# Strassen weight combinations on VectorE in portions, a re-dealt last round, and a later start for the second token group's operands

## The chip, the cores and the metric

The kernel runs on one core of one Trainium2 chip. The metric is the device time of one execution in microseconds. Three runs of the kernel before took 757.85, 758.66 and 759.13 us; the median is 758.66 us. One more execution was profiled, and all rows below come from it.

## The reference

An attention with packed queries makes 2304 rows of 512 values; two feed-forward networks follow, the first with softplus, the second with x·sigmoid(x). Everything is float32.

```python
p_packed = sm_attn(p, k, v)                 # per batch and head
x = sm_attn(q, p_packed, p_packed)          # then [2304, 512]
h = x @ moe_w_in                            # 512 -> 2048
x = softplus(h) @ moe_w_out                 # 2048 -> 512
h = x @ moe2_w_in
out = (h * sigmoid(h)) @ moe2_w_out
```

## The kernel before, in words

Each float32 operand of a large product is split into a high part (rounded to the matmul's fp32r format by a ScalarE copy) and a low part (the difference, by VectorE); a product is three matmuls: low×high, high×low, high×high.

The first 380 us do the attention and the first network. The second network (`second`) runs in 24 steps, `step(k)`: 8 steps for each of three groups of 768 tokens, which is two blocks of 384. Its input product is a Winograd-Strassen scheme with seven products Q1 to Q7 per step (`products`, L900, six matmuls each), into four PSUM tiles pA, pB, pC and pD. Several products accumulate into one tile with VectorE or ScalarE reading the tile in between: pA receives Q1, is read as `ta` (L1091), then receives Q2; pB receives Q6, is read by VectorE as `u2` (rows show `tu`), then receives Q7; pC receives Q5, is read for `c2`, then receives Q3. So a late reader stops TensorE. The order on TensorE in a step is Q1, Q6, output 0, Q2, Q7, output 1, Q5, output 2, Q3, Q4, output 3. An output is a 12-matmul block of the output product two steps earlier (`out_tile`, L1039).

The seven operand tiles of a token group's x lie in the pools `xc0` and `xc1` (alternating). `x_high` (ScalarE, L569), `x_low` (VectorE, L573) and `x_sum` (VectorE, L566) fill them in the last two steps before the group's first step; the table `plans` in `plan_second` gives each piece a step and a point. `xc1` is opened in the place of the pool `stage` when step 6 begins, and `stage` holds the last converted weights (`whl`) until their DMA to the scratch tensor `wd` (`store_i`, L237) has read them.

For the last group the output product is also a Strassen scheme. Its weight combinations are computed once: eight tiles of 128 × 2048 are loaded from `od` (`t_load`, L804), combined by GpSimd (`t_sums`, L808: one sum over 128 × 1024, then four differences over 128 × 256), split (`t_high` on ScalarE, L817; `t_low` on VectorE, L821) and stored to `td` (`t_store`, L825). `T_AT` gives each tile its step (16 is added) and says whether it follows `T_EARLY` or `T_LATE`, the tables of points. Tiles 0 to 5 use the pool `tw`, the others the first 512 columns of `ya`.

A point is a place in the program text of a step: L, A0 and D0 stand after `u2`, D1, A1 and M after Q7 and the low part of g11, D2 after the first read of pC, A2 after output 2, S before output 3's add, A3 and D3 at the end. All engines execute in program order, SyncE's DMA issues too, so a piece at a point waits behind what is written before it and holds up what is written after.

From step 18 on, fourteen output blocks per pair of steps (`out_group`, L965, six matmuls; seven accumulators in two halves d) are added into `ya` by `add_group` (L976, GpSimd's part L977). A block uses one of four PSUM banks, so TensorE runs at most four blocks ahead of the adds. The sums of the second operand (`s_sum` L941, `s_high` L945, `s_low` L949) are GpSimd's and ScalarE's in the steps. After step 23 the last sums and the last fourteen blocks (f = 3) follow; here `add_group` combines the accumulators: GpSimd adds Q1 to Q6 and Q2, Q5 to Q3, Q6 to Q7 and Q3; VectorE adds the PSUM block, and for Q7 makes two outputs by operations on `ya` alone; each finished output is sent by SyncE (L983).

```python
elif q == Q1:
    vec(a[q], y, a[q])
    gps(a[Q6], a[Q6], a[Q1])
    gps(a[Q2], a[Q2], a[Q1])
```

Of the kernel before, what the change touches and what calls it, by code (L numbers as in the profile page):

```python
# [13 lines left out]
ALU = mybir.AluOpType  # L14
# [4 lines left out]
B, H, S, D = 4, 8, 576, 64  # L19
# [8 lines left out]
D1 = D + 1  # L28
# [13 lines left out]
NQ = 7  # L42
RI = 5
Q1, Q6, Q2, Q7, Q5, Q3, Q4 = range(NQ)
# [5 lines left out]
def body(ctx, tc, kT, vv, qT, pT, wi1, wo1, wi2, wo2, out):  # L50
    nc = tc.nc
# [744 lines left out]
    B_OF = {Q1: (0, 0), Q2: (1, 0), Q3: (1, 1)}  # L796

    def t_load(n):
        if n < 6:
            t = st["tw"].tile([P, 4, DM], F32, name="tw", bufs=5)  # L800
        else:
            t = ya[:, :, :DM]
        ts[n] = t.rearrange("p (c h) (a n) -> p c h a n", c=2, a=2), t
        nc.sync.dma_start(out=t, in_=od[:, n * 4 * DM:(n + 1) * 4 * DM].rearrange("p (c n) -> p c n", c=4))  # L804

    def t_sums(n):
        w, t = ts[n][0][:, :, 0], ts[n][0][:, :, 1]
        op = lambda o, a, b, op: nc.gpsimd.tensor_tensor(out=o, in0=a, in1=b, op=op)  # L808
        at = lambda i: t[:, i[0], i[1]]
        op(w, w, t, ALU.add)  # L810
        op(at(T1), w[:, 0, 1], w[:, 0, 0], ALU.subtract)
        op(at(T3), w[:, 1, 1], w[:, 0, 1], ALU.subtract)
        op(at(T2), w[:, 1, 1], at(T1), ALU.subtract)
        op(at(T4), at(T2), w[:, 1, 0], ALU.subtract)

    def t_high(n):
        nc.scalar.activation(out=ts[n][0][:, :, 0].bitcast(F32R), in_=ts[n][0][:, :, 1], func=AF.Copy)  # L817
# [6 lines left out]
        v = td[:, n * 4 * DM:(n + 1) * 4 * DM].rearrange("p (c n) -> p c n", c=4)  # L824
        nc.sync.dma_start(out=v, in_=ts.pop(n)[1])  # L825

    T_AT = (-8, 0), (-8, 1), (-7, 1), (-6, 0), (-5, 0), (-5, 1), (-4, 0), (-1, 0)
    T_EARLY = (0, "M", t_load), (1, "D0", t_sums), (1, "A2", t_high), (1, "D3", t_low), (2, "A0", t_store)
    T_LATE = (0, "S", t_load), (1, "D2", t_sums), (2, "A0", t_high), (2, "D1", t_low), (2, "M", t_store)

    ring_s = {}

# [11 lines left out]
    def plan_second():  # L844
        for n in range(NJ):
            s, late = T_AT[n]
            s += SO * NJ
            for ds, point, fn in T_LATE if late else T_EARLY:
                fill(s + ds, point, fn, n)
        for jp in range(4, NJ):  # L850
            k = jp - 2
            for n in 2 * jp, 2 * jp + 1:
                fill(k - 1, "M", load_raw, "i", n, 0)
                fill(k, "A0", scale_raw, "i", n, True)
                fill(k, "D0", plain_i, n, True)
            fill(k, "D1", sums_i)
            fill(k, "A1", high_i, 0, 4)
            fill(k, "A1", high_i, 4, NQ)
            fill(k, "D2", low_i, 0, 4)
            fill(k, "D2", low_i, 4, NQ)  # L860
            fill(k, "S", store_i, jp)
        for s in range(1, NSUP):
            plans = {
                (0, "D0"): ((x_high, Q1), (x_high, Q2)),
                (0, "D1"): ((x_high, Q4), (x_low, Q1)),
                (0, "D2"): ((x_low, Q2), (x_low, Q4)),
                (0, "D3"): ((x_sum, Q5),),
                (1, "D0"): ((x_high, Q5), (x_sum, Q7)),
                (1, "D1"): ((x_low, Q5), (x_sum, Q6), (x_high, Q7), (x_high, Q6)),
                (1, "D2"): ((x_low, Q7), (x_low, Q6)),  # L870
                (1, "D3"): ((x_sum, Q3),),
                (2, "D0"): ((x_high, Q3),),
                (2, "D1"): ((x_low, Q3),),
            }
            for (h, point), fns in plans.items():
                for fn, q in fns:
                    fill(NJ * s - 2 + h, point, fn, s, q)

    def second():
# [1 line left out]
        pb = pool("pb", 1, space=PSUM)  # L881
        tmp = st["tmp"]
        slots = [*range(6)]
        units, opnd, saved, later = [], {}, {}, {}
        tw_stack = ExitStack()
        G = None
        gs1, frees = {}, {}
# [46 lines left out]
        def s_sum(k, q, eng):  # L934
            g11, c12, c2 = saved[k]
            s1, s2 = sum_of(Q5), sum_of(Q6)
            a, b, op = {
                Q5: (c2[:, 0], c2[:, 1], ALU.add), Q7: (g11, c2[:, 0], ALU.subtract),
                Q6: (s1, g11, ALU.subtract), Q3: (c12, s2, ALU.subtract),
            }[q]  # L940
            eng.tensor_tensor(out=sum_of(q), in0=a, in1=b, op=op)  # L941
# [8 lines left out]

        def acc(q, d):
            n = 2 * OUT_ORDER.index(q) + d
            c = n // 4 * N1
            return ya[:, n % 4, c:c + N1]

# [16 lines left out]
        def add_group(f, n, y):  # L972
            i, d = divmod(n, 2)
            q = OUT_ORDER[i]
            a = {x: acc(x, d) for x in OUT_ORDER}
            vec = lambda o, x, z, op=ALU.add: nc.vector.tensor_tensor(out=o, in0=x, in1=z, op=op)  # L976
            gps = lambda o, x, z, op=ALU.add: nc.gpsimd.tensor_tensor(out=o, in0=x, in1=z, op=op)  # L977
            yout = lambda t, h: ya[:, 2 * h + d, (2 * SO + t) * N1:(2 * SO + t + 1) * N1]

            def send(t, h):  # L980
                c = (2 * SO + t) * N1
                dm = 2 * h + d
                nc.sync.dma_start(out=out[dm * P:(dm + 1) * P, c:c + N1], in_=yout(t, h))  # L983

            if not f:
                if d:
                    nc.vector.tensor_copy(a[q], y)
                else:
                    nc.scalar.activation(out=a[q], in_=y, func=AF.Copy)
            elif f < NPASS - 1:  # L990
                vec(a[q], y, a[q])
            elif q == Q1:
                vec(a[q], y, a[q])
                gps(a[Q6], a[Q6], a[Q1])
                gps(a[Q2], a[Q2], a[Q1])
            elif q == Q4:
                vec(a[q], y, a[q])
            elif q == Q5:
                vec(a[q], y, a[q])
                gps(a[Q3], a[Q3], a[Q5])  # L1000
            elif q == Q6:
                vec(a[q], y, a[q])
                gps(a[Q7], a[Q7], a[Q6])
                later.setdefault(Q6, []).append(lambda: gps(a[Q3], a[Q3], a[Q6]))
                if d:
                    for fn in later.pop(Q6):
                        fn()
            elif q == Q7:
                vec(a[q], y, a[q])
                vec(yout(1, 0), a[q], a[Q4], ALU.subtract)  # L1010
                send(1, 0)
                vec(yout(1, 1), a[q], a[Q5])
                send(1, 1)
            elif q == Q3:
                vec(yout(0, 1), y, a[q])
                send(0, 1)
            else:
                vec(yout(0, 0), y, a[q])
                send(0, 0)
# [199 lines left out]
                open_xc(1, side="right", reuse_waits="tile")  # L1219
            step(k)  # L1220
        k = NSTEP
        for q in Q5, Q6:
            s_sum(k - 1, q, nc.vector)
            s_high(k - 1, q)
            s_low(k - 1, q, nc.vector)
        for q in Q7, Q3:
            s_sum(k - 1, q, nc.gpsimd)
            s_high(k - 1, q)
            s_low(k - 1, q, nc.gpsimd)
        for k in NSTEP, NSTEP + 1:  # L1230
            for n in range(NQ):
                group_of(k, n)

    setup()
    with tc.manual_schedule():
# [53 lines left out]
```

## Time and profile before

| What | Value |
|---|---|
| Median of three runs | 758.66 us |
| The profiled execution's own time | 758.51 us |
| Its span, first to last instruction | 756.7 us |
| TensorE busy | 739.3 us, 98% of the span |
| VectorE busy | 531.6 us, 70% |
| ScalarE busy | 382.8 us, 51% |
| GpSimd busy | 126.4 us, 17% |
| Mean granted TensorE clock | 0.995 of full speed |

The profiled execution takes 1.8 us longer than its span and lies 0.15 us under the median. Busy shares are averages over very different stages; what matters for a change is which wait ended last at the place that it touches.

### The profile page before, as it was taken

How to read it: one execution, taken by the hardware profiler on the slowest of the kernel's cores; microseconds unless marked ns; L12 is line 12 of the kernel's file. 1: busy time of each engine (PE TensorE's matmuls, PEld its weight loads, DVE VectorE, ACT ScalarE, POOL GpSimd, SP SyncE). 2: the span in 40 equal slices, each digit the busy share in tenths (PEclk: the TensorE clock that was granted, in tenths of full speed). 3: DMA queues.
4: the chain of work that ended last, by engine and by line, in shares of the span. 5: the costliest groups of instructions: out<-in, count | busy, mean ns of one | idle time of the engine just before them, and what ended most of it. 6: DMA issues, size and time to landing. Idle time of an engine off the chain costs nothing.

```text
span 756.7 us, 13739 instructions
## 1 busy us (share of the span) xinstructions
PE 739.3 (98%) x5440; PEld 704.9 (93%) x5440; DVE 531.6 (70%) x962; ACT 382.8 (51%) x723; POOL 126.4 (17%) x116
## 2 busy tenths in 40 slices
PE   8999999999999999999999999999989999999996
PEld 6777889999999999999999998999989999999995
DVE  3888887879877997897556775755467675445555
ACT  3677786656555565565445453333434333543430
POOL 0000000000000000000000000045363035466546
PEclk9999999999999999999999999999999999999998
DMA  9965033145444352567268888689999677987732
GB/s 338 339 218 183 1 140 113 56 181 189 178 165 181 140 195 85 205 241 271 61 234 320 349 290 322 231 288 345 355 392 318 233 257 252 340 268 241 228 108 84
DMA packets 55744, 169.01 MB, mean 223 GB/s; under 512 B 5248, under 2 KB 23168, under 8 KB 52608
## 3 DMA queue, kind: packets, MB, share of 16 engines
q1 hardware_dynamic: 55680, 168.13, 62.5%
q8 instruction: 43, 0.70, 0.4%
q14 instruction: 21, 0.17, 0.1%
HBM read 131.93 MB, written 36.18 MB: 222 GB/s over the span
## 4 chain that ended last, share of the span: by engine, by line
PE 85%; DMA 4%; ACT 4%; DVE 3%; issue 1%; POOL 1%; SPq 1%; DVEq 0%; ACTq 0%; POOLq 0%
PE y L527 24%; PE y L1039 16%; PE h L487 12%; PE pC L900 6%; PE y L965 6%; PE pB L900 6%; PE pA L900 6%; PE pD L900 3%; DMA wraw<-wo 3%; PE psa L453 2%; PE y L520 2%; DMA wd<-whl 2%; POOL ya L977 1%; PE psa L360 1%; DVE ya L976 1%
## 5 line engine op out<-in xcount | busy, mean ns | idle before, releaser
L527 PE MATMUL y<-gh,w 128*128 128x288 f32 x960 | 212.1, 296 | 0.3 <-DVE ya L542 0.2
L527 PEld LDWEIGHTS y<-gh,w 128*128 128x128 f32 x960 | 160.3, 188 | 13.0 <-issue 5.5
L1039 PE MATMUL y<-G,w 128*128 128x384 f32 x768 | 143.2, 334 | 0.0
L527 PE MATMUL y<-gl,w 128*128 128x288 f32 x480 | 141.8, 295 | 0.1
L1039 PEld LDWEIGHTS y<-G,w 128*128 128x128 f32 x768 | 134.0, 188 | 0.0
L487 PE MATMUL h<-ax,vw 128*128 128x288 f32 x768 | 125.0, 298 | 0.3 <-DVE ax L436 0.3
L808 POOL TENSOR_TENSOR tw<-tw 128x256 f32<-128x256 f32 (+1 forms) x30 | 36.9, 1245 | 525.4 <-DMA yT<-ya 498.9
L487 PEld LDWEIGHTS h<-ax,vw 128*128 128x128 f32 x768 | 109.3, 188 | 2.4 <-DVE ax L436 0.5
L527 PEld LDWEIGHTS y<-gl,w 128*128 128x128 f32 x480 | 90.2, 188 | 0.5 <-DVE gl L504 0.5
L499 ACT ACTIVATE gt<-h 128x288 f32<-128x288 f32 x120 | 48.5, 404 | 68.6 <-PE h L487 64.0
L504 DVE TENSOR_TENSOR gl<-gt,gh 128x288 fp32r<-128x288 f32 x120 | 54.1, 451 | 25.1 <-ACT gh L500 24.3
L900 PE MATMUL pB<-xc,w 128*128 128x384 f32 x288 | 57.9, 335 | 2.0 <-DVE tu L1073 1.9
L900 PE MATMUL pC<-xc,w 128*128 128x384 f32 x288 | 57.7, 334 | 1.8 <-DVE c L1073 1.8
L1157 ACT ACTIVATE tc<-tc 128x384 f32<-128x384 f32 x24 | 12.6, 526 | 90.6 <-DVE tc L1073 90.6
L900 PE MATMUL pA<-xc,w 128*128 128x384 f32 x288 | 57.8, 335 | 0.1
L1073 DVE TENSOR_TENSOR tu<-ta,pB 128x384 f32<-128x384 f32 x48 | 26.5, 551 | 42.9 <-PE pB L900 38.2
L500 ACT ACTIVATE gh<-gt 128x288 fp32r<-128x288 f32 x120 | 53.4, 445 | 3.8
L900 PEld LDWEIGHTS pB<-xc,w 128*128 128x128 f32 x288 | 50.5, 188 | 2.7 <-DVE tu L1073 2.7
L900 PEld LDWEIGHTS pC<-xc,w 128*128 128x128 f32 x288 | 50.5, 188 | 2.2 <-DVE c L1073 2.2
L544 DVE TENSOR_TENSOR ya<-y,ya 128x288 f32<-128x288 f32 x104 | 46.8, 451 | 7.2 <-PE y L527 7.0
L900 PEld LDWEIGHTS pA<-xc,w 128*128 128x128 f32 x288 | 50.5, 188 | 0.4 <-ACT ta L1091 0.4
L1052 DVE TENSOR_TENSOR ya<-y,ya 128x384 f32<-128x384 f32 x48 | 26.6, 554 | 25.4 <-PE y L1039 25.3
(122 smaller groups left out, 1098.0 us busy)
## 6 DMA issues: line engine op xcount, KB each, us to landing
w<-wd SPq DMA_DIRECT2D x84, 512.0 KB, 4.8
w<-od SPq DMA_DIRECT2D x32, 512.0 KB, 6.8
wd<-whl SPq DMA_DIRECT2D x8, 1792.0 KB, 7.1
wraw<-wi SPq DMA_DIRECT2D x16, 512.0 KB, 5.6
wraw<-wo SPq DMA_DIRECT2D x16, 512.0 KB, 6.3
raw<-wi SPq DMA_DIRECT2D x16, 512.0 KB, 6.1
raw<-wo SPq DMA_DIRECT2D x16, 512.0 KB, 6.8
od<-ohl SPq DMA_DIRECT2D x16, 512.0 KB, 3.1
```

The costliest lines, as they stand in the source:

```text
L487: nc.tensor.matmul(h, lhsT=w, rhs=x, start=(i == 0), stop=(i == len(mm) - 1))
L499: nc.scalar.activation(out=gt, in_=h, func=AF.Softplus)
L500: nc.scalar.activation(out=gh, in_=gt, func=AF.Copy)
L504: nc.vector.tensor_tensor(out=gl, in0=gt, in1=gh.bitcast(F32), op=ALU.subtract)
L527: nc.tensor.matmul(y, lhsT=w[:, c], rhs=g, start=(j == js[0] and m == 0), stop=(j == js[-1] and m == 2))
L544: nc.vector.tensor_tensor(out=acc, in0=y, in1=acc, op=ALU.add)
L808: op = lambda o, a, b, op: nc.gpsimd.tensor_tensor(out=o, in0=a, in1=b, op=op)
L900: nc.tensor.matmul(out, lhsT=a, rhs=b, start=start and not i, stop=not start and i == len(mm) - 1, skip_group_check=True,)
L965: nc.tensor.matmul(y, lhsT=w[:, j, a, c], rhs=g[:, h], start=(j == m == 0), stop=(j == 1 and m == 2))
L1039: nc.tensor.matmul(y, lhsT=a[:, c], rhs=G[:, g, h, j], start=(k % 2 == j == m == 0), stop=(k % 2 == j == 1 and m == 2),)
L1052: nc.vector.tensor_tensor(out=acc, in0=y, in1=acc, op=ALU.add)
L1073: add = lambda o, i, j, op=ALU.add: nc.vector.tensor_tensor(out=o, in0=i, in1=j, op=op)
```

## The change

Four edits stand in the diff. First, `t_sums` is cut into `t_plain`, `t_sums1` and `t_sums2`, all on VectorE instead of GpSimd, each at a point of its own; `T_AT`, `T_EARLY` and `T_LATE` are new, and tiles 3, 6 and 7 lie in `ya` (tile 3 lay in `tw`; `t_load(n)` for the other five uses `tw`). Second, `plans` begins the x operands of the second and third token group at D2 of the step two ahead, not at D0 (for the second group that is step 6). Third, after step 23 the sums and low parts of Q6, Q7 and Q3 are dealt anew: GpSimd keeps one sum, VectorE takes the rest and does them between its adds; GpSimd's `Q2 += Q1` of the second half goes to the end of its row. Fourth, the accumulators of the last group's outputs are moved round by eight places in `ya`, which goes with the places of the tiles.

```diff
--- before.py
+++ after.py
@@ -796,22 +796,29 @@
     B_OF = {Q1: (0, 0), Q2: (1, 0), Q3: (1, 1)}
 
     def t_load(n):
-        if n < 6:
+        if n not in (3, 6, 7):
             t = st["tw"].tile([P, 4, DM], F32, name="tw", bufs=5)
         else:
             t = ya[:, :, :DM]
         ts[n] = t.rearrange("p (c h) (a n) -> p c h a n", c=2, a=2), t
         nc.sync.dma_start(out=t, in_=od[:, n * 4 * DM:(n + 1) * 4 * DM].rearrange("p (c n) -> p c n", c=4))
 
-    def t_sums(n):
+    def t_op(o, a, b, op=ALU.subtract):
+        nc.vector.tensor_tensor(out=o, in0=a, in1=b, op=op)
+
+    def t_plain(n):
         w, t = ts[n][0][:, :, 0], ts[n][0][:, :, 1]
-        op = lambda o, a, b, op: nc.gpsimd.tensor_tensor(out=o, in0=a, in1=b, op=op)
-        at = lambda i: t[:, i[0], i[1]]
-        op(w, w, t, ALU.add)
-        op(at(T1), w[:, 0, 1], w[:, 0, 0], ALU.subtract)
-        op(at(T3), w[:, 1, 1], w[:, 0, 1], ALU.subtract)
-        op(at(T2), w[:, 1, 1], at(T1), ALU.subtract)
-        op(at(T4), at(T2), w[:, 1, 0], ALU.subtract)
+        t_op(w, w, t, ALU.add)
+
+    def t_sums1(n):
+        w, t = ts[n][0][:, :, 0], ts[n][0][:, :, 1]
+        t_op(t[:, 0, 0], w[:, 0, 1], w[:, 0, 0])
+        t_op(t[:, 0, 1], w[:, 1, 1], w[:, 0, 1])
+
+    def t_sums2(n):
+        w, t = ts[n][0][:, :, 0], ts[n][0][:, :, 1]
+        t_op(t[:, 1, 0], w[:, 1, 1], t[:, 0, 0])
+        t_op(t[:, 1, 1], t[:, 1, 0], w[:, 1, 0])
 
     def t_high(n):
         nc.scalar.activation(out=ts[n][0][:, :, 0].bitcast(F32R), in_=ts[n][0][:, :, 1], func=AF.Copy)
@@ -824,9 +831,15 @@
         v = td[:, n * 4 * DM:(n + 1) * 4 * DM].rearrange("p (c n) -> p c n", c=4)
         nc.sync.dma_start(out=v, in_=ts.pop(n)[1])
 
-    T_AT = (-8, 0), (-8, 1), (-7, 1), (-6, 0), (-5, 0), (-5, 1), (-4, 0), (-1, 0)
-    T_EARLY = (0, "M", t_load), (1, "D0", t_sums), (1, "A2", t_high), (1, "D3", t_low), (2, "A0", t_store)
-    T_LATE = (0, "S", t_load), (1, "D2", t_sums), (2, "A0", t_high), (2, "D1", t_low), (2, "M", t_store)
+    T_AT = (-8, 0), (-8, 1), (-7, 0), (-6, 0), (-6, 1), (-5, 0), (-4, 0), (0, 0)
+    T_EARLY = (
+        (0, "M", t_load), (1, "D0", t_plain), (1, "D1", t_sums1), (1, "D2", t_sums2),
+        (1, "A2", t_high), (1, "S", t_low), (2, "A0", t_store),
+    )
+    T_LATE = (
+        (0, "S", t_load), (1, "D2", t_plain), (1, "S", t_sums1), (2, "D0", t_sums2),
+        (2, "A1", t_high), (2, "D2", t_low), (2, "S", t_store),
+    )
 
     ring_s = {}
 
@@ -861,14 +874,13 @@
             fill(k, "S", store_i, jp)
         for s in range(1, NSUP):
             plans = {
-                (0, "D0"): ((x_high, Q1), (x_high, Q2)),
-                (0, "D1"): ((x_high, Q4), (x_low, Q1)),
-                (0, "D2"): ((x_low, Q2), (x_low, Q4)),
-                (0, "D3"): ((x_sum, Q5),),
-                (1, "D0"): ((x_high, Q5), (x_sum, Q7)),
-                (1, "D1"): ((x_low, Q5), (x_sum, Q6), (x_high, Q7), (x_high, Q6)),
-                (1, "D2"): ((x_low, Q7), (x_low, Q6)),
-                (1, "D3"): ((x_sum, Q3),),
+                (0, "D2"): ((x_high, Q1), (x_high, Q4)),
+                (0, "S"): ((x_low, Q1), (x_low, Q4)),
+                (0, "A3"): ((x_high, Q2),),
+                (1, "D0"): ((x_sum, Q5), (x_sum, Q7), (x_low, Q2)),
+                (1, "D1"): ((x_sum, Q6), (x_high, Q6), (x_high, Q5)),
+                (1, "D2"): ((x_high, Q7), (x_low, Q6), (x_low, Q5)),
+                (1, "S"): ((x_low, Q7), (x_sum, Q3)),
                 (2, "D0"): ((x_high, Q3),),
                 (2, "D1"): ((x_low, Q3),),
             }
@@ -881,7 +893,7 @@
         pb = pool("pb", 1, space=PSUM)
         tmp = st["tmp"]
         slots = [*range(6)]
-        units, opnd, saved, later = [], {}, {}, {}
+        units, opnd, saved, later = [], {}, {}, []
         tw_stack = ExitStack()
         G = None
         gs1, frees = {}, {}
@@ -950,6 +962,7 @@
 
         def acc(q, d):
             n = 2 * OUT_ORDER.index(q) + d
+            n = (n + 8) % 14
             c = n // 4 * N1
             return ya[:, n % 4, c:c + N1]
 
@@ -992,7 +1005,10 @@
             elif q == Q1:
                 vec(a[q], y, a[q])
                 gps(a[Q6], a[Q6], a[Q1])
-                gps(a[Q2], a[Q2], a[Q1])
+                if not d:
+                    gps(a[Q2], a[Q2], a[Q1])
+                else:
+                    later.append(lambda: gps(a[Q2], a[Q2], a[Q1]))
             elif q == Q4:
                 vec(a[q], y, a[q])
             elif q == Q5:
@@ -1001,9 +1017,9 @@
             elif q == Q6:
                 vec(a[q], y, a[q])
                 gps(a[Q7], a[Q7], a[Q6])
-                later.setdefault(Q6, []).append(lambda: gps(a[Q3], a[Q3], a[Q6]))
+                later.insert(d, lambda: gps(a[Q3], a[Q3], a[Q6]))
                 if d:
-                    for fn in later.pop(Q6):
+                    for fn in later:
                         fn()
             elif q == Q7:
                 vec(a[q], y, a[q])
@@ -1219,17 +1235,25 @@
                 open_xc(1, side="right", reuse_waits="tile")
             step(k)
         k = NSTEP
-        for q in Q5, Q6:
-            s_sum(k - 1, q, nc.vector)
-            s_high(k - 1, q)
-            s_low(k - 1, q, nc.vector)
-        for q in Q7, Q3:
-            s_sum(k - 1, q, nc.gpsimd)
-            s_high(k - 1, q)
-            s_low(k - 1, q, nc.gpsimd)
-        for k in NSTEP, NSTEP + 1:
-            for n in range(NQ):
-                group_of(k, n)
+        s_sum(k - 1, Q7, nc.gpsimd)
+        s_sum(k - 1, Q5, nc.vector)
+        s_high(k - 1, Q5)
+        s_sum(k - 1, Q6, nc.vector)
+        s_high(k - 1, Q7)
+        s_low(k - 1, Q5, nc.vector)
+        s_high(k - 1, Q6)
+        s_sum(k - 1, Q3, nc.vector)
+        s_high(k - 1, Q3)
+        group_of(k, 0)
+        s_low(k - 1, Q6, nc.vector)
+        group_of(k, 1)
+        s_low(k - 1, Q7, nc.vector)
+        group_of(k, 2)
+        s_low(k - 1, Q3, nc.vector)
+        for n in range(3, NQ):
+            group_of(k, n)
+        for n in range(NQ):
+            group_of(k + 1, n)
 
     setup()
     with tc.manual_schedule():
```

How the instructions stand, at three places. ScalarE, steps 6 and 7, from `ta` of step 6 (`xc` are the second group's operands, `tg` and `tc` the step's own activations). Before:

```order
L1091 ACTIVATE ta<-pA 128x384
L569 ACTIVATE xc_5806<-ya 128x768 x2
L1115 ACTIVATE tg_5814<-pA 128x384
L1116 ACTIVATE G<-tg_5814 128x384
L569 ACTIVATE xc_5806<-ya 128x768
L1157 ACTIVATE tc_5815<-tc_5815 128x384
```

Now:

```order
L1107 ACTIVATE ta<-pA 128x384
L1131 ACTIVATE tg_5814<-pA 128x384
L1132 ACTIVATE G<-tg_5814 128x384
L569 ACTIVATE xc_5806<-ya 128x768 x2
L1173 ACTIVATE tc_5815<-tc_5815 128x384
L1174 ACTIVATE G<-tc_5815 128x384
L1177 ACTIVATE c_5816<-c_5816 128x768
L1179 ACTIVATE G<-c_5816 128x768
L569 ACTIVATE xc_5806<-ya 128x768
```

The first two splits now follow the activations of g11 (`tg` and `G<-tg`) instead of preceding them; the third has moved to the end of the step.

VectorE, from the end of step 11 into step 12 (`tw` are the weight tiles, `tu` is the first or second read of pB, `c` a read of pC or pD). Before:

```order
L1073 TENSOR_TENSOR G<-tc_6692,G 128x384
L1052 TENSOR_TENSOR ya<-y,ya 128x384
L1073 TENSOR_TENSOR G<-c_6693,G 128x768
L821 TENSOR_TENSOR tw<-tw 128x2x512
L1073 TENSOR_TENSOR tu_6836<-ta,pB 128x384
L1052 TENSOR_TENSOR ya<-y,ya 128x384
L1073 TENSOR_TENSOR tu_6837<-ta,pB 128x384
```

Now:

```order
L1089 TENSOR_TENSOR G<-tc_6546,G 128x384
L828 TENSOR_TENSOR ya<-ya 128x2x512
L807 TENSOR_TENSOR tw<-tw 128x256 x2
L1089 TENSOR_TENSOR G<-c_6547,G 128x768
L1089 TENSOR_TENSOR tu_6691<-ta,pB 128x384
L807 TENSOR_TENSOR tw<-tw 128x256 x2
L807 TENSOR_TENSOR tw<-tw 128x2x512
L1068 TENSOR_TENSOR ya<-y,ya 128x384
L1089 TENSOR_TENSOR tu_6692<-ta,pB 128x384
```

The low part of a weight tile (L821, now L828) no longer stands between the last low part of step 11 and the first read of pB; portions of the combinations stand before and behind that read.

VectorE after step 23 (`sums` by L941 are the operand sums, `G` and `xs` by L949 their low parts, `ya<-y,ya` the adds of blocks). Before:

```order
L941 TENSOR_TENSOR sums<-c_8351 128x384
L949 TENSOR_TENSOR G<-sums,G 128x384
L941 TENSOR_TENSOR sums<-sums,tg_8349 128x384
L949 TENSOR_TENSOR G<-sums,G 128x384
L976 TENSOR_TENSOR ya<-y,ya 128x384 x9
L976 TENSOR_TENSOR ya<-ya 128x384 x2
```

Now:

```order
L953 TENSOR_TENSOR sums<-c_8350 128x384
L953 TENSOR_TENSOR sums<-sums,tg_8348 128x384
L961 TENSOR_TENSOR G<-sums,G 128x384
L953 TENSOR_TENSOR sums<-tc_8349,sums 128x384
L989 TENSOR_TENSOR ya<-y,ya 128x384
L961 TENSOR_TENSOR xs<-sums,xs 128x384
L989 TENSOR_TENSOR ya<-y,ya 128x384
L961 TENSOR_TENSOR G<-sums,G 128x384
L989 TENSOR_TENSOR ya<-y,ya 128x384
L961 TENSOR_TENSOR xs<-sums,xs 128x384
L989 TENSOR_TENSOR ya<-y,ya 128x384 x6
L989 TENSOR_TENSOR ya<-ya 128x384 x2
```

VectorE now does one more sum and two more low parts here, dealt between the first four adds; GpSimd's ten additions of accumulators follow its one sum directly.

## Rows read from the trace of the kernel before

**Rows 1.** The page, part 1: busy time, share of the span and instructions of each engine.
```profile
PE 739.3 (98%) x5440; PEld 704.9 (93%) x5440; DVE 531.6 (70%) x962; ACT 382.8 (51%) x723; POOL 126.4 (17%) x116
```
**Rows 2.** Waits of TensorE: releaser, us in total, times, longest.
```profile
PE y L965 <- DVE ya L976: 3.6, 3, 1.8
PE pB L900 <- DVE tu L1073: 1.9, 1, 1.9
PE pC L900 <- DVE c L1073: 1.8, 1, 1.8
```
**Rows 3.** Chain of waits, 540 to 575 us: start, us, what.
```profile
557.74 2.08 PE y L1039 x12
```
**Rows 4.** Timeline, steps 5 and 6: start, us, instructions [idle before, releaser].
```profile
445.19 1.55 DVE L221 TENSOR_TENSOR wf<-wf 128x256 f32<-128x256 f32 x4
...
454.08 0.95 DVE L1073 TENSOR_TENSOR G<-c,G 128x768 fp32r<-128x768 f32 x1
...
461.89 1.58 ACT L569 ACTIVATE xc<-ya 128x768 fp32r<-128x768 f32 x2 [6.75 <-DMA wd<-whl]
...
462.77 2.25 PE L1039 MATMUL y<-G,w 128*128 128x384 f32 x12
...
466.25 0.54 DVE L1073 TENSOR_TENSOR c<-tu,pC 128x384 f32<-128x384 f32 x1
...
466.85 1.31 PE L900 MATMUL pC<-xc,w 128*128 128x384 f32 x6 [1.83 <-DVE c L1073]
```
**Rows 5.** Timeline, steps 12 and 13.
```profile
551.45 2.79 DVE L1073 TENSOR_TENSOR G<-c,G 128x768 fp32r<-128x768 f32 x1 [3.00 <-ACT G L1163]
...
553.27 1.20 PE L900 MATMUL pA<-xc,w 128*128 128x384 f32 x6
554.16 1.74 DVE L821 TENSOR_TENSOR tw<-tw 128x1024 fp32r<-128x1024 f32 x1
...
556.43 1.31 PE L900 MATMUL pB<-xc,w 128*128 128x384 f32 x6 [1.95 <-DVE tu L1073]
...
571.10 1.20 PE L900 MATMUL pA<-xc,w 128*128 128x384 f32 x6
...
572.40 1.31 PE L900 MATMUL pB<-xc,w 128*128 128x384 f32 x6
...
574.69 1.22 DVE L821 TENSOR_TENSOR tw<-tw 128x1024 fp32r<-128x1024 f32 x1
```
**Rows 6.** GpSimd's instructions by line and shape: count | busy, mean ns | idle before.
```profile
L808 POOL TENSOR_TENSOR tw<-tw 128x1024 f32<-128x1024 f32 x6 | 14.4, 2402 | 524.5 <-DMA yT<-ya 498.9 <-DMA tw<-od 23.3 <-DMA w<-od 2.3
```
**Rows 7.** DMA issues, 490 to 600 us: count, KB each, median us to landing.
```profile
tw<-od SPq DMA_DIRECT2D x6, 1024.0 KB, 7.9
...
ya<-od SPq DMA_DIRECT2D x1, 1024.0 KB, 8.8
td<-ya SPq DMA_DIRECT2D x1, 1024.0 KB, 7.3
```
**Rows 8.** A 20 us window: engines' busy us (count), granted clock, DMA share, GB/s.
```profile
520.00:540.00 20.00, 20.00 (x117) 20.00 (x117) 7.53 (x12) 8.48 (x16) 9.68 (x8) 1.00 1.01 399
```
**Rows 9.** Timeline from the end of step 23.
```profile
730.59 2.76 PE L965 MATMUL y<-xs,w 128*128 128x384 f32 x15
...
732.87 0.56 DVE L976 TENSOR_TENSOR ya<-y,ya 128x384 f32<-128x384 f32 x1 [0.32 <-PE y L965]
...
734.39 0.53 ACT L945 ACTIVATE G<-sums 128x384 fp32r<-128x384 f32 x1 [1.61 <-DVE sums L941]
...
737.65 4.95 PE L965 MATMUL y<-G,w 128*128 128x384 f32 x27 [0.66 <-DVE ya L976]
...
740.61 10.30 POOL L977 TENSOR_TENSOR ya<-ya 128x384 f32<-128x384 f32 x10
...
748.04 2.02 DVE L976 TENSOR_TENSOR ya<-ya 128x384 f32<-128x384 f32 x2
...
751.73 1.94 DVE L976 TENSOR_TENSOR ya<-y,ya 128x384 f32<-128x384 f32 x4
```

## The prediction

> **What bounds the kernel now.** I read the page first: TensorE is busy for 739.3 of 756.7 us [rows 1], so a change that leaves its instructions alone can only win back idle time, some 17 us, most of it in the start that this diff does not touch. The waits of TensorE [rows 2] name what is left in the second network: reads of pB and pC by VectorE, and the adds of the last round. The chain of waits gives the unit: 12 matmuls take 2.08 us [rows 3], so six take 1.04, a step 7 × 1.04 + 4 × 2.08 = 15.6 us. Then the timelines show where each wait comes from.
>
> *Step 6.* Output 1 begins at 462.77 and should hand over to Q3 into pC at 464.85; Q3 begins at 466.85, and its six matmuls show 1.31 busy instead of the usual 1.20 [rows 4, 5]: 2.0 + 0.1 = 2.1 us lost. VectorE read pC only at 466.25, because ScalarE had stood for 6.75 us before two operand splits, until the weights' DMA out of the place of `xc1` had landed at 461.89 [rows 4]; the activations that VectorE needs stand behind those splits.
>
> *Steps 12 and 13.* Q2 begins at 553.27, so Q7 into pB is due at 554.31 and begins at 556.43: 2.1 + 0.1 = 2.2 us. At the second place it is due at 572.14 and begins at 572.40: 0.3 + 0.1 = 0.4 us [rows 5]. What is late there is VectorE: a low part of 128 × 768 took 2.79 us where the same form took 0.95 in step 6 [rows 4, 5], and a weight tile's low part 1.74 us where it took 1.22 later [rows 5]. Both slow ones fall on GpSimd's combinations, whose large sum holds for 2.40 us [rows 6].
>
> *The last round.* Step 23's last twelve matmuls begin at 730.59, so the fourteen blocks begin at 732.67 and need 14.6 us, until 747.2. VectorE's last add ends at 751.73 + 1.94 = 753.67, and the span 3.07 us later [rows 9]. Between them stand GpSimd's ten additions, 10.30 us from 740.61 on [rows 9], which began only when GpSimd had done its share of the operand sums.
>
> **The change part by part.**
>
> *Operands half a step later.* ScalarE now does g11's activations before the two splits. The DMA lands as before, at 461.9; the splits end at 463.5, and ScalarE's next necessary work is c12 after Q3, near 466. The 2.1 us go. The split moved to the end of a step (half of 1.58, 0.8 us [rows 4]) stands before the copy of pA, which then ends about 2.6 us into the step and is due at 4.16. No operand becomes late: the low part of Q7 is written in the step before its use. Gain 2.1, bounds 0 and 2.1.
>
> *Combinations on VectorE.* Removed from GpSimd: 8 × 5 instructions. Added to VectorE: per tile one sum over 128 × 1024, for which I take 1.22 us from the low part of the same size, and four differences over 128 × 256, 1.55 us together [rows 4, 5]; upper bound 1.74 for the large one where GpSimd still works (step 17). A step has on VectorE eleven pieces of about 0.55 and one of 0.95, 7.0 us. The fullest steps get a whole tile (1.22 + 1.55 + 1.22 = 4.0) and half of another (2.0): 13.0 of 15.6 us. Order matters more than the sum: with portions before the last low part, VectorE reads pB at about 3.3 us into a step, and TensorE needs this at 5.2; 1.9 us are spare. With GpSimd silent, the 2.79 is 0.95 again. Both stalls go: gain 2.6, bounds 0 and 2.6. The tiles' loads, stores and splits are the same in number; loads 2, 4 and 5 are issued half a step earlier, load 7 a step later. SyncE waits at load 6 for the store of tile 3, since both now lie in `ya`; weight loads behind it are issued some 3 us later, and each was issued more than a step before its use. I cost this at nothing; a rival below prices it. The accumulators' new places cost nothing: the outputs and the tile that lay there left steps earlier.
>
> *The last round.* I walk the queues with 0.55 us for a VectorE piece (0.47 where pieces follow each other, half of 0.95), and 0.94 for a GpSimd addition: its ten took 10.30, of which two pieces of VectorE's 2.02 pair held up 0.45 each [rows 9]. The unknown is what VectorE pays for an operation on `ya` or the operand sums alone while GpSimd adds: that pair took 2.02 instead of 0.95 [rows 4, 9]. I take strict turns. VectorE: two sums, the low part of Q5 (ScalarE's high part was ready at 734.92 [rows 9]) and a third sum until 736.0, the first add until 736.4; from there GpSimd starts, four us earlier than before. With the three low parts in turns with GpSimd's first additions, the first four adds end at 736.4, 737.4, 738.7 and 740.1; the banks keep TensorE nearly free (0.2 us). GpSimd adds Q5 by 742.5, Q6 to Q7 by 743.4 and 744.4. VectorE adds Q7's first block at 744.0; its four operations on `ya` alone alternate with GpSimd's last three additions until 748.9; four more adds end at 750.75. So the gain is 753.67 − 750.75 = 2.9 us. Bounds: without any turns VectorE follows TensorE, 747.2 + 0.2 for the lag of an add [rows 9] + 0.55 = 748.0, gain 5.7; with each GpSimd addition at 1.3 us, 752.5, gain 1.2; and 0 if something unseen holds the row. The 2.02 pair is the nearest row and speaks for turns.
>
> The page "SBUF — State Buffer" of the Trainium skill, section "SBUF: two separate sides", says that VectorE and GpSimd share a port pair as an exclusive lock, held for a whole instruction, also against VectorE operations with two SBUF inputs. By it the sum of the last round is the 2.9 above; by the opposite, free sharing, 5.7. The stretched 2.79 agrees [rows 5].
>
> *Sum.* 2.1 + 2.6 + 2.9 = 7.6 us off the profiled execution's 758.51: **750.9 us**. That execution lies 0.15 under the median of the runs, less than a run's scatter. A measurement here can tell about 0.2%, 1.5 us, from no change.
>
> **The rivals.**
>
> *A free last round.* VectorE's pieces hardly meet GpSimd's: gain 5.7 there, 748.1 us. For it: adds from PSUM keep 0.56 beside GpSimd [rows 9]. Against: seven pieces do not read PSUM.
>
> *VectorE becomes the bound of the last round.* It has three pieces more, and turns stretch both engines: gain 0 to 1.2 there, 752.6 to 753.8 us.
>
> *A stall stays or is replaced.* The edit to `plans` might only move ScalarE's wait, or step 17, where GpSimd's operand sums still run, might hold VectorE before pB or pC. Each is worth about 2 us: 753.0 us. Against the first: 2.5 us lie between the splits' end and ScalarE's next necessary work.
>
> *VectorE waits for DMA: slower.* A queue that the reads of pB and pC share now stands behind landings, where only GpSimd stood before; GpSimd waited 23.3 us for these loads [rows 6]. Place: steps 9 to 13. A late tile (1 and 4) is issued near the end of a step and read 10.1 us into the next, about 10.7 us for a landing of 7.9 in the median [rows 7]; with 1.9 spare it decides at 12.6. Tile 6 waits for a store of 7.3 and a load of 8.8 [rows 7]; from about 3 us into step 12 it lands 3.5 us into step 13, and may come until 6.7. If landings doubled, tiles 1 and 4 cost 3.2 each, tile 6 16.1 − 3.2 = 12.9: 19.3 us, 770.2 us. For it: the DMA engines are full, 399 GB/s [rows 8], and three loads come earlier. Against: the landings above were measured in that very stretch, and the bytes are the same.
>
> **How the numbers follow.** The forecast, three stalls gone and a last round in turns (749.8 to 752.2): 60%. Free last round: 14%. VectorE bound there: 14%. A stall stays: 9%. Waits for DMA: 3%. The range from 748.1 to 753.9 takes in the bounds of the last round and one stall, and leaves the worse cases out. All but the last, and a mix of the last two that eats 6 us or more, are faster by over 0.2%: 0.95; within 0.2%: 0.02; slower: 0.03.
>
> **What the profile afterwards would show.** Right: TensorE without a gap between Q7's predecessor and Q7 in steps 9 to 13 and before Q3 in step 6; the 128 × 768 low part near 0.95 there; no GpSimd before step 17; GpSimd's ten additions starting near 736.5 less the 4.7 us won before; VectorE's operations on `ya` alone at about 1 us each, and VectorE's last add some 3 us after TensorE's last matmul. Wrong: VectorE waiting for `od`, TensorE's gaps at other reads, or a last round whose end has not come nearer to step 23.

## The result and the profile after

The changed kernel takes 750.65 us in the median of four runs (750.31 to 751.14); the kernel before took 758.25 in four runs (757.20 to 759.13). The ratio is 0.9901, with a 95% interval from 0.9884 to 0.9918: 7.6 us faster. The profiled execution took 750.44 us with a span of 748.3.

The page, part 1, of the kernel after (busy time, share of the span, instructions), against [rows 1]:

```profile
PE 737.3 (99%) x5440; PEld 705.2 (94%) x5440; DVE 545.3 (73%) x1005; ACT 382.7 (51%) x723; POOL 75.8 (10%) x73
```

GpSimd has lost 43 instructions and 50.6 us, VectorE has gained 43 and 13.7 us. TensorE's instructions are the same in number; of the 8.4 us that the span lost, 6.4 were its idle time, and its mean granted clock is 0.999 against 0.995, of which the last section says more. The waits of TensorE after (engine, line, what it waited for: us in total, times, longest):

```profile
PE y L662 <- POOL ident masks.py:199: 1.4, 1, 1.4
PE psa L360 <- ACT et L352: 1.0, 2, 0.6
PE psa L345 <- ACT e L336: 0.9, 1, 0.9
PE y L520 <- ACT gf L493: 0.8, 1, 0.8
PE psa L408 <- ACT pt L397: 0.5, 1, 0.5
PE h L487 <- DVE ax L436: 0.3, 1, 0.3
PE y L527 <- DVE ya L542: 0.2, 1, 0.2
```

Against [rows 2], the entries of the second network (pB, pC and the adds of the last blocks) have left the list. What remains belongs to the first 380 us. The list is of the matmuls; their weight loads (PEld) still wait 0.23 and 0.45 us for VectorE in the last round, the second of which is among the rows below.

*Step 6*, in the timeline after (start, us, engine, line, operation; in brackets the idle time before it and what ended it):

```profile
458.24 0.49 ACT L1131 ACTIVATE tg<-pA 128x384 f32<-128x384 f32 x1 [3.67 <-PE pA L912]
...
461.65 1.58 ACT L569 ACTIVATE xc<-ya 128x768 fp32r<-128x768 f32 x2 [2.36 <-DMA wd<-whl]
...
462.40 0.56 DVE L1089 TENSOR_TENSOR c<-tu,pC 128x384 f32<-128x384 f32 x1 [0.48 <-PE pC L912]
...
464.28 1.20 PE L912 MATMUL pC<-xc,w 128*128 128x384 f32 x6
```

ScalarE still waits for the DMA out of `stage`, which lands as before, but for 2.36 us instead of 6.75 [rows 4], and g11's activations (`tg`) are done by then. VectorE stands idle for 0.48 us until TensorE has filled pC, and Q3's six matmuls show the usual 1.20.

*Step 12* begins at 546.46:

```profile
545.72 1.22 DVE L828 TENSOR_TENSOR ya<-ya 128x1024 fp32r<-128x1024 f32 x1
546.46 1.20 PE L912 MATMUL pA<-xc,w 128*128 128x384 f32 x6
...
548.79 0.96 DVE L1089 TENSOR_TENSOR G<-c,G 128x768 fp32r<-128x768 f32 x1 [1.19 <-ACT G L1179]
...
549.67 0.55 DVE L1089 TENSOR_TENSOR tu<-ta,pB 128x384 f32<-128x384 f32 x1
550.13 2.02 DVE L807 TENSOR_TENSOR tw<-tw 128x256 f32<-128x256 f32 x3
...
550.62 1.20 PE L912 MATMUL pA<-xc,w 128*128 128x384 f32 x6
...
551.65 0.51 PE L912 MATMUL pB<-xc,w 128*128 128x384 f32 x2
```

The low part that took 2.79 us [rows 5] takes 0.96; pB has been read 3.76 us into the step, and Q7 begins at 551.65, right behind Q2. The whole sum on VectorE takes 1.22 us, the third of the three L807 pieces here.

*The last round* begins at 727.41:

```profile
731.27 11.77 POOL L990 TENSOR_TENSOR ya<-ya 128x384 f32<-128x384 f32 x10 [3.14 <-DVE ya L989]
...
738.25 0.56 DVE L989 TENSOR_TENSOR ya<-y,ya 128x384 f32<-128x384 f32 x1 [1.50 <-POOL ya L990]
...
738.84 2.05 DVE L989 TENSOR_TENSOR ya<-ya 128x384 f32<-128x384 f32 x2
...
741.39 2.06 DVE L989 TENSOR_TENSOR ya<-ya 128x384 f32<-128x384 f32 x2
741.41 0.48 PEld L978 LDWEIGHTS y<-G,w 128*128 128x128 f32 x3 [0.45 <-DVE ya L989]
...
742.05 0.69 PE L978 MATMUL y<-xs,w 128*128 128x384 f32 x3
743.38 1.94 DVE L989 TENSOR_TENSOR ya<-y,ya 128x384 f32<-128x384 f32 x4
```

GpSimd's ten additions begin 3.9 us into the round, where [rows 9] had them at 740.61 − 732.67 = 7.9. VectorE's last add ends at 743.38 + 1.94 = 745.32, 17.9 us into the round; before it was 753.67 − 732.67 = 21.0.

So the two traces differ by this much: steps 6 to 13 took 582.91 − 453.41 = 129.5 us before and 577.65 − 452.84 = 124.8 after (the first matmuls of steps 6 and 14), 4.7 us less and exactly eight times 15.6; the last round 3.1 us less; and 0.6 us lie before step 6, where nothing was changed.

### The profile page after: what moved, and what is told of

The parts are those of the page before. It is cut to its first block, busy times and chain, and to the rows that moved or that the text cites. A ratio compares the mean times of both kernels' runs of the same rounds, so it can differ in the third digit from the quotient of the medians.

```text
span 748.3 us, 13730 instructions
## 1 busy us (share of the span) xinstructions
PE 737.3 (99%) x5440; PEld 705.2 (94%) x5440; DVE 545.3 (73%) x1005; ACT 382.7 (51%) x723; POOL 75.8 (10%) x73
## 4 chain that ended last, share of the span: by engine, by line
PE 89%; ACT 4%; DVE 3%; DMA 1%; issue 1%; SPq 1%; POOL 0%; DVEq 0%; ACTq 0%
PE y L527 25%; PE y L1055 18%; PE h L487 13%; PE pC L912 7%; PE pA L912 7%; PE pB L912 7%; PE y L978 6%; PE pD L912 3%; PE psa L453 2%; PE y L520 2%; DMA wraw<-wo 1%; DVE ya L989 1%; PE psa L360 1%; PE psa L408 1%; ACT e L336 1%
## 5 line engine op out<-in xcount | busy, mean ns | idle before, releaser
L953 POOL TENSOR_TENSOR sums<-c 128x384 f32<-128x384 f32 x7 | 7.8, 1115 | 644.8 <-DMA yT<-ya 622.8
L912 PEld LDWEIGHTS pB<-xc,w 128*128 128x128 f32 x288 | 50.6, 188 | 0.0
L1173 ACT ACTIVATE tc<-tc 128x384 f32<-128x384 f32 x24 | 12.6, 525 | 67.7 <-DVE tc L1089 67.5
L1131 ACT ACTIVATE tg<-pA 128x384 f32<-128x384 f32 x24 | 11.8, 492 | 64.8 <-PE pA L912 64.8
```

The costliest lines, as they stand in the source:

```text
L912: nc.tensor.matmul(out, lhsT=a, rhs=b, start=start and not i, stop=not start and i == len(mm) - 1, skip_group_check=True,)
```

## The experiments

Each part was tried alone on the kernel before, then the causes were taken apart. Times are medians of the runs; a ratio is to runs of the kernel before on the same chip. The first four share 33 such runs (758.65 us in the median).

**Only the later x operands.** The edit is the new `plans` table of the diff, nothing else.

```diff
-                (0, "D0"): ((x_high, Q1), (x_high, Q2)),
...
+                (0, "D2"): ((x_high, Q1), (x_high, Q4)),
...
```

> The kernel before with the new table of operand pieces alone. Theory (three separate stalls that add up): ScalarE's wait for the DMA shrinks from 6.75 to about 2.4 us and holds nothing up; TensorE's 2.1 us gap before Q3 in step 6 is gone, the two gaps of steps 12 and 13 stay, the last round is as before: 2.1 us faster, about 756.2 against 758.3. Rival (the wait only moves, or the stall reappears where the queues meet next): 0 to 0.5 us faster. Third possibility (the gap only hides a later one): step 7 or 8 shows a new gap.

756.43 us, ratio 0.9964 (0.9945 to 0.9983). In its trace step 6 has no gap, and the ones of steps 12 and 13 stay (1.8 and 0.7 us lost). The first term stands by itself.

**Only the combinations on VectorE.** The edit is `t_load`, the three functions `t_plain`, `t_sums1`, `t_sums2`, the three tables and the line in `acc`.

```diff
-        if n < 6:
+        if n not in (3, 6, 7):
...
-        op = lambda o, a, b, op: nc.gpsimd.tensor_tensor(out=o, in0=a, in1=b, op=op)
...
+            n = (n + 8) % 14
```

> The kernel before with the weight combinations on VectorE in portions, their new steps and the accumulators' new places, nothing else. Theory: the gaps of steps 12 and 13 go, the one of step 6 (2.1 us) and the last round stay: 2.6 us faster, about 755.7. Rival (VectorE's extra 20 us make new gaps in steps 9 to 13, which the earlier operand start hid in the whole change): less than 1 us faster.

755.19 us, ratio 0.9955 (0.9938 to 0.9972). There is no gap in steps 12 and 13. The traced execution is the slowest of its twelve runs (757.82 us), and its step 6 shows something more; TensorE there:

```profile
467.03 1.34 PE L913 MATMUL pC<-xc,w 128*128 128x384 f32 x6 [2.55 <-DVE c L1087]
468.20 1.79 PE L913 MATMUL pD<-xc,w 128*128 128x384 f32 x6
469.78 3.27 PE L1053 MATMUL y<-G,w 128*128 128x384 f32 x12
472.89 1.20 PE L913 MATMUL pA<-xc,w 128*128 128x384 f32 x6
```

and the windows of 460 to 480 us (busy time and instructions of PE, PEld, DVE, ACT, POOL, then the granted TensorE clock, the DMA share and GB/s), of this kernel first and of the whole change second:

```profile
460.00:480.00 20.00, 17.45 (x92) 17.14 (x91) 10.99 (x18) 8.86 (x14) 0.00 (x0) 0.91 0.74 271
```

```profile
460.00:480.00 20.00, 20.00 (x117) 20.00 (x116) 14.81 (x23) 8.86 (x13) 0.00 (x0) 1.00 0.80 303
```

Behind the gap the granted clock was at the lower of its two levels for a while (0.50, which is 1.2 GHz, in the windows from 469 to 472 us): twelve matmuls take 3.27 instead of 2.24 us, six 1.79 instead of 1.20. The step took 20.0 instead of 15.6 us, 2.8 for the gap and 1.6 for the clock.

**Only the last round.** The edit is the code behind step 23 and the lines with `later`.

```diff
-        for q in Q5, Q6:
-            s_sum(k - 1, q, nc.vector)
...
+        s_sum(k - 1, Q7, nc.gpsimd)
+        s_sum(k - 1, Q5, nc.vector)
...
```

> The kernel before with the re-dealt last round alone. Theory (turns between VectorE and GpSimd): from the start of the last round to VectorE's last add 18.0 us instead of 21.0, all gaps before stay: 3.0 us faster, about 755.3. Rival (the last round gains only because it begins differently after the other edits): 1 us or less.

755.09 us, ratio 0.9954 (0.9933 to 0.9974); the round takes 17.9 us in its trace, as in the whole change. The third term stands by itself too.

The three medians lie 2.2, 3.5 and 3.6 us under the 758.65, where 2.1, 2.6 and 3.0 were expected. Each expectation lies inside the interval of its ratio, but runs of one kernel are spread over 3 to 7 us here, so the sizes of the terms rest on the traces and not on these medians.

**Only the place of a low part.** GpSimd keeps the combinations; in the kernel before one word changes.

```diff
-    T_EARLY = (0, "M", t_load), (1, "D0", t_sums), (1, "A2", t_high), (1, "D3", t_low), (2, "A0", t_store)
+    T_EARLY = (0, "M", t_load), (1, "D0", t_sums), (1, "A2", t_high), (1, "S", t_low), (2, "A0", t_store)
```

> The kernel before with one word changed: the low part of an early weight tile stands before the last low part of the step, as in the change, but the combinations stay on GpSimd. Theory (GpSimd's running combination stretches the 128 x 768 low part): that part still takes about 2.8 us, but nothing of 1.74 us stands behind it any more, so the gap of step 12 shrinks from 2.2 to about 0.4 us and that of step 13 goes: about 2.0 us faster. Rival A (the place of the low part was everything): both gaps go, 2.6 us faster. Rival B (GpSimd was everything, the place nothing): both gaps stay, no change.

755.89 us, ratio 0.9952 (0.9934 to 0.9970). Step 12 begins at 548.69 here:

```profile
547.95 1.22 DVE L821 TENSOR_TENSOR tw<-tw 128x1024 fp32r<-128x1024 f32 x1
...
550.54 6.00 POOL L808 TENSOR_TENSOR tw<-tw 128x1024 f32<-128x1024 f32 x5 [7.34 <-DMA tw<-od]
...
551.03 2.72 DVE L1073 TENSOR_TENSOR G<-c,G 128x768 fp32r<-128x768 f32 x1 [1.86 <-ACT G L1163]
...
553.67 0.54 DVE L1073 TENSOR_TENSOR tu<-ta,pB 128x384 f32<-128x384 f32 x1
...
554.27 1.32 PE L900 MATMUL pB<-xc,w 128*128 128x384 f32 x6 [0.21 <-DVE tu L1073]
```

The low part of 128 × 768 is as slow as ever beside GpSimd, 2.72 us, but the weight tile's low part (L821) now stands ahead of it, in time in which VectorE had nothing to do. Steps 12 and 13 lose 0.5 us instead of 2.6. So most of what I had put down to a silent GpSimd came from the order of VectorE's own queue.

**The whole change with GpSimd's combinations kept.** This is the kernel before with the new `plans`, the new last round and that one word; against the changed kernel it is this, with `t_load`, `t_sums`, `T_AT`, `T_LATE` and `acc` as before:

```diff
-        nc.vector.tensor_tensor(out=o, in0=a, in1=b, op=op)
...
+        op = lambda o, a, b, op: nc.gpsimd.tensor_tensor(out=o, in0=a, in1=b, op=op)
...
+    T_EARLY = (0, "M", t_load), (1, "D0", t_sums), (1, "A2", t_high), (1, "S", t_low), (2, "A0", t_store)
```

It ran beside the changed kernel itself, which was repeated, and 11 runs of the kernel before (759.31 us in the median).

> The kernel before with the later operands, the new last round and the low part of an early weight tile placed sooner, but the combinations left on GpSimd in their old steps. Theory (two causes in steps 12 and 13: the place of the low part gave 2.1 us of 2.6, GpSimd's share the last 0.5): within 0.7 us of the whole change, gaps of 0.5 us or less. Rival (with the 2 us of step 6 won, the steps meet GpSimd's work at another point and VectorE's portions are needed): gaps of 1 to 2 us return, 1 to 2 us slower than the whole change.

> The changed kernel once more, as the mark for the others of this call: about 7.6 us faster than before, no gap of TensorE in steps 6 to 23, its operand read of pB ready at about 3.8 us into step 12.

750.48 us (six runs, 750.28 to 751.03; ratio 0.9886, 0.9864 to 0.9909) without the move, 750.56 (six runs, 750.34 to 750.96; ratio 0.9887, 0.9866 to 0.9907) with it: no difference. Steps 6 to 13 of the kernel without it take 578.02 − 453.22 = 124.8 us, no gap either. Step 12, from 546.82:

```profile
547.89 8.68 POOL L808 TENSOR_TENSOR tw<-tw 128x1024 f32<-128x1024 f32 x6 [6.78 <-DMA tw<-od]
...
549.16 1.95 DVE L1075 TENSOR_TENSOR G<-c,G 128x768 fp32r<-128x768 f32 x1 [1.86 <-ACT G L1165]
...
551.03 0.54 DVE L1075 TENSOR_TENSOR tu<-ta,pB 128x384 f32<-128x384 f32 x1
...
552.02 1.20 PE L899 MATMUL pB<-xc,w 128*128 128x384 f32 x6
```

The read of pB ends at 551.57, 0.45 us before Q7. In the whole change it ends at 550.22 and Q7 begins at 551.65, 1.4 us. The move buys slack, not time.

**The portions on GpSimd.** In the changed kernel `t_op` uses GpSimd; places and tables stay.

```diff
-        nc.vector.tensor_tensor(out=o, in0=a, in1=b, op=op)
+        nc.gpsimd.tensor_tensor(out=o, in0=a, in1=b, op=op)
```

> The changed kernel with the combinations given back to GpSimd, all places and steps as in the change. Theory (turns): the 128 x 768 low parts that meet a combination take 2.5 to 2.8 us instead of 0.95, but reads of pB still come in time or miss it by less than 0.7 us. Rival (GpSimd is slower, a tile's five pieces take 7 us, and the splits become late): VectorE waits for low parts at S, gaps of 1 us and more.

One run: 751.05 us. One gap of this kind came back, 0.8 us in step 11, a little more than the 0.7 that the theory allowed and less than the rival's 1:

```profile
533.14 5.18 POOL L807 TENSOR_TENSOR ya<-ya 128x1024 f32<-128x1024 f32 x4 [11.54 <-DMA ya<-od]
...
533.33 3.02 DVE L1089 TENSOR_TENSOR G<-c,G 128x768 fp32r<-128x768 f32 x1 [1.86 <-ACT G L1179]
...
536.88 1.32 PE L912 MATMUL pB<-xc,w 128*128 128x384 f32 x6 [0.52 <-DVE tu L1089]
```

Here the large sum and the low part begin together, the low part takes 3.02 us, and pB is read too late. GpSimd's lengthening does cost time, then, where the places leave no slack for it. One run alone cannot tell its time from the changed kernel's.

**The last additions left out.** In the changed kernel the loop over `later` goes.

```diff
-                if d:
-                    for fn in later:
-                        fn()
```

> The changed kernel without GpSimd's last three additions (Q3 += Q6 of both halves, Q2 += Q1 of the second half), so part of the output lacks a term. It measures the price of turns in the last round. Theory: VectorE's two pairs of operations on ya alone take 0.95 to 1.4 us each instead of 2.05, the first one still meeting an addition, and VectorE's last add ends 1.5 to 2.2 us earlier relative to the start of the last round (17.9 us in the change). Rival (VectorE is held by TensorE's blocks or the banks, not by GpSimd): less than 0.5 us.

One run: 748.64 us; the last add comes 16.0 us into the round, 1.9 sooner. VectorE, with GpSimd silent from 739.5 on:

```profile
738.57 0.56 DVE L989 TENSOR_TENSOR ya<-y,ya 128x384 f32<-128x384 f32 x1 [1.49 <-POOL ya L990]
...
739.17 1.23 DVE L989 TENSOR_TENSOR ya<-ya 128x384 f32<-128x384 f32 x2
...
740.90 1.03 DVE L989 TENSOR_TENSOR ya<-ya 128x384 f32<-128x384 f32 x2
```

The pairs take 1.23 and 1.03 us instead of 2.05 and 2.06. So the turns are there, and the last round still pays 1.9 us for them.

**Two attempts to win that back, both misses.** First, `Q2 += Q1` of the first half also goes behind GpSimd's other additions; second, VectorE does it in its 1.5 us of waiting.

```diff
-                if not d:
-                    gps(a[Q2], a[Q2], a[Q1])
-                else:
-                    later.append(lambda: gps(a[Q2], a[Q2], a[Q1]))
+                later.append(lambda: gps(a[Q2], a[Q2], a[Q1]))
```

> The changed kernel, with GpSimd's addition Q2 += Q1 of the first half moved behind its others as well. In the changed kernel VectorE idles 1.5 us at 738.25 for GpSimd's Q7 += Q6, and TensorE then loses 0.4 us because no bank is free. Theory (in the last round the order of GpSimd's queue counts, and each of its ten additions holds what is behind it for 1.18 us): Q7 comes 1.2 us sooner, TensorE's 0.4 gap goes, VectorE's last add ends about 1.1 us earlier relative to the round's start (16.8 instead of 17.9 us), the time is 749.5. Rival (turns only move from one pair to the other, GpSimd's end sets the round): the round stays at 17.9 us, 750.6, or gets longer since Q2's first block now waits for GpSimd's ninth addition: up to 0.6 us slower, 751.2.

```diff
-                if not d:
-                    gps(a[Q2], a[Q2], a[Q1])
-                else:
+                if d:
                     later.append(lambda: gps(a[Q2], a[Q2], a[Q1]))
...
                 if d:
+                    vec(acc(Q2, 0), acc(Q2, 0), acc(Q1, 0))
                     for fn in later:
```

> The changed kernel, with the addition Q2 += Q1 of the first half done by VectorE, behind its add of Q6's second block, where it idles 1.5 us in the changed kernel; GpSimd keeps nine additions. Theory: the piece costs VectorE about 1 us in turns, of idle time; GpSimd reaches Q7 += Q6 1.2 us sooner and ends 1.2 us sooner, so VectorE's second pair on ya meets it less; the last add ends 1.3 to 1.7 us earlier relative to the round's start (16.2 to 16.6 instead of 17.9 us), 749.1 us. Rival (the piece takes VectorE as long as GpSimd gains): no change, 750.6 us.

750.85 us (five runs, 750.24 to 752.22) and 751.12 us (five runs, 750.52 to 751.33); the rounds take 17.9 and 18.2 us. The theory fell, and the first one's trace says why:

```profile
733.05 2.55 POOL L990 TENSOR_TENSOR ya<-ya 128x384 f32<-128x384 f32 x2 [3.15 <-DVE ya L989]
...
737.03 9.04 POOL L990 TENSOR_TENSOR ya<-ya 128x384 f32<-128x384 f32 x8 [1.43 <-DVE ya L989]
...
740.02 0.56 DVE L989 TENSOR_TENSOR ya<-y,ya 128x384 f32<-128x384 f32 x1 [1.49 <-POOL ya L990]
```

GpSimd, freed of one addition, only waits 1.43 us for VectorE's adds of Q5: the two `Q3 += Q5` stand before `Q7 += Q6` in its row, and VectorE waits for the latter.

**The row of GpSimd in another order.** `Q3 += Q5` goes behind `Q7 += Q6`, and `Q2 += Q1` back in its row.

```diff
-                if not d:
-                    gps(a[Q2], a[Q2], a[Q1])
-                else:
-                    later.append(lambda: gps(a[Q2], a[Q2], a[Q1]))
+                gps(a[Q2], a[Q2], a[Q1])
...
-                gps(a[Q3], a[Q3], a[Q5])
+                later.append(lambda: gps(a[Q3], a[Q3], a[Q5]))
...
-                later.insert(d, lambda: gps(a[Q3], a[Q3], a[Q6]))
+                later.insert(2 * d + 1, lambda: gps(a[Q3], a[Q3], a[Q6]))
```

> The changed kernel, with GpSimd's two additions Q3 += Q5 moved behind Q7 += Q6, and Q2 += Q1 of the second half back in its row (it fills the time until Q6 is added). In the changed kernel and in both attempts before, VectorE waited for Q7 += Q6 until 10.8 to 11.2 us into the round, whatever was done about Q2, because Q3 += Q5 starts only after Q5's second add and stands before it. Theory (that chain through the row of GpSimd sets the end): Q7 += Q6 of the first half starts right behind Q6's first add, 8.8 us into the round, ends at 9.9; VectorE's wait shrinks from 1.5 to about 0.5 us, TensorE's gap of 0.3 to 0.6 us later in the round goes, VectorE's last add ends 0.9 us sooner: 17.0 instead of 17.9 us, 749.7 us. Rival (the ten additions with their turns set the end, in whatever order): 17.9 us, 750.6.

749.99 us (six runs, 749.75 to 750.52); ratio 0.9881 (0.9860 to 0.9903), with the kernel before at 759.39 in the median of 11. Its round begins at 727.75:

```profile
731.61 12.03 POOL L990 TENSOR_TENSOR ya<-ya 128x384 f32<-128x384 f32 x10 [3.14 <-DVE ya L989]
...
737.58 0.56 DVE L989 TENSOR_TENSOR ya<-y,ya 128x384 f32<-128x384 f32 x1 [0.48 <-POOL ya L990]
...
742.72 0.54 DVE L989 TENSOR_TENSOR ya<-y,ya 128x384 f32<-128x384 f32 x1
743.68 1.49 DVE L989 TENSOR_TENSOR ya<-y,ya 128x384 f32<-128x384 f32 x3 [0.42 <-POOL ya L990]
```

VectorE's wait before Q7 shrinks from 1.50 to 0.48 us, and of the two short waits of TensorE's weight loads the later one, 0.45 us, is gone. The round takes 743.68 + 1.49 − 727.75 = 17.4 us, half of the gain expected: VectorE, sooner at Q3's second block, waits 0.42 us for the last of GpSimd's ten. This is the fastest kernel measured, some 0.6 us under the changed kernel; the two ran on different chips and their runs overlap a little, so the 0.5 us in the round is the firmer number.

## Why the prediction was right

**Step 6.** Forecast: 2.1 us, by activations that no longer stand behind the wait. Measured: a step of 15.6 us instead of 17.7 before. The DMA landed at 461.65 us (forecast 461.9).

**Steps 12 and 13.** Forecast: 2.6 us, with the two stalls gone. The two terms together measured 4.7. The sizes taken for VectorE's pieces held: 1.22 us for the large sum, 0.75 for two differences, 0.96 for the undisturbed low part. pB was read 3.8 us into the step, where the walk had it at 3.3. One reason was given too much weight. "With GpSimd silent, the 2.79 is 0.95 again" is true, but it decides nothing: the 2.79 us may stay if the weight tile's low part is out of the way. The one word was worth 2.1 of the 2.6 us, and with the other edits all of them. The sentence before, that order matters more than the sum, was the better one.

**The last round.** Forecast: 2.9 us, with turns; measured: 3.1. The first four adds were to end 3.7, 4.7, 6.0 and 7.4 us into the round; they ended after 3.8, 4.7, 6.0 and 7.3. GpSimd's additions took 1.01 us alone, where the walk had 0.94, and up to 1.33 beside VectorE, 11.77 for the ten, and VectorE's operations on `ya` alone about a microsecond each. That GpSimd's share is dealt in turns was a choice between bounds of 5.7 and 1.2 us for the gain; leaving three additions out showed it, 2.05 us for a pair against 1.03. This agrees with the Trainium skill's page "SBUF — State Buffer", section "SBUF: two separate sides", by which whichever of the two engines starts first holds their shared ports for its whole instruction. The adds from PSUM, 0.54 to 0.56 us also beside GpSimd, were not held.

**The sum.** 750.9 us was forecast and 750.65 measured; in the profiled executions the three terms gave 7.8 us, where 7.6 were forecast. These executions lie 758.51 − 750.44 = 8.1 us apart; the other 0.3 us belongs to no term. In the repeat the medians lie 759.31 − 750.56 = 8.75 us apart. The forecast starts from one execution of a kernel whose runs are spread over 7 us, so its agreement to 0.25 us is partly luck; that of the three terms is not.

**The signs.** In steps 9 to 13 the 128 × 768 low part took 0.95 to 0.96 us and TensorE had no gap, GpSimd's first instruction after the setup came at 624.1 us, at the turn to step 17, and its ten additions began at 731.27 us, where 736.5 − 4.7 = 731.8 was named.

**The rivals.** The free last round (748.1) and VectorE as its bound (752.6 or more) are excluded by the 17.9 us; no stall stayed. The slower one, VectorE waiting for DMA, did not come: in the second network VectorE waited for no DMA. Its premise, longer landings, came for one load. Over 480 to 570 us the five loads into `tw` took 7.9 us in the median, as before, and the late tiles 1 and 4, which the rival named, landed after 7.4 and 9.9 us, under its limit of 12.6. Landings in the stretch of 530 to 570 us (issue, KB each, median us to landing):

```profile
td<-tw SPq DMA_DIRECT2D x3, 1024.0 KB, 13.0
...
tw<-od SPq DMA_DIRECT2D x1, 1024.0 KB, 13.2
...
ya<-od SPq DMA_DIRECT2D x1, 1024.0 KB, 5.4
```

The load of 13.2 us is that of tile 5. It was issued at 536.62 us and had landed at 549.8; its first reader, the large sum, ends with the L807 group at 552.15 and so began at 550.9, 1.1 us later. Tile 6 did wait for tile 3's store (SyncE stood for 5.5 us), but its load took 5.4 us and landed 2.1 us into step 13, against a forecast of 3.5 and a limit of 6.7. So VectorE came within about a microsecond of waiting at tile 5, with the DMA engines 0.93 busy from 540 to 560 us. How much later TensorE would have stalled was not tried.

## What to carry to other kernels

Before work is moved from one engine to another, look at what stands in the late engine's own queue ahead of the instruction that is waited for: taking one piece out of its way cost one word here and, beside the other edits, gave as much as the move of forty instructions. Where two engines add into the same buffers, follow the chain through both rows; taking work off an engine won nothing as long as an addition that could not start yet stood ahead of the one that was waited for, and putting these in another order did. Measure the last stage from its own start, since what the stages before win only shifts it.

## What the runs showed of the hardware

A gap in TensorE's work can cost more than its length. In the trace of the combinations alone, 2.7 us without a matmul in step 6 were followed by a fall of the granted clock from 1.00 to 0.50 (from 2.4 to 1.2 GHz), and 18 matmuls took 1.6 us more than usual. In the same step of the kernel before, 2.0 us without a matmul were followed by no fall. There the clock fell in the last round, behind a gap of 1.8 us: it was 0.60 in the window of 749 to 750 us and 0.50 from there to the end. That is where the trace's mean of 0.995 comes from; all windows of steps 6 to 13 show 1.00. Three of its last matmuls took 1.33 us, but VectorE worked without a pause from 747.45 us on, so this fall shows no cost.

In the trace of the whole change no matmul ran at the lower level. The runs fit that: the kernel before scatters from 755.1 to 762.6 us, the longer runs mostly at the lower mean clocks (0.999 down to 0.991); the changed kernel and the one with GpSimd's combinations kept lie each within a microsecond, at 0.997 to 0.999. That falls behind the gaps make this scatter was not traced run by run, and so is not shown.

With the gaps gone, the next wait that shows is one of TensorE in step 6 for a DMA that loads weights (`w` from `wd`): 0.3, 0.3 and 1.0 us lost in three of the eight traces of the changed kernel and its variants, and nothing in the others. Two executions of one and the same kernel, the changed one, are among them, one with 0.3 us and one with nothing, so the edits do not decide it.
